# Delta-rule attention: the merge's first and second products in steps of their own, and stage_d by kind of product

## The chip, the cores and the metric

The kernel runs on one core of one Trainium2 chip. The metric is the device time in microseconds of one execution; before the change the median of three runs is 844.51 us (843.97 to 844.6). Engines are named as in the profile: PE multiplies matrices, PEld loads its weights, DVE and ACT do elementwise work, POOL fills memory, SP issues most transfers.

## The reference

Three parts follow one another: a delta-rule attention over 4 batches, 8 heads, 768 positions and head size 48; a block with Fourier transforms and a two-layer network; and a gated block. Only the first is touched:

```python
k_n = k / (np.linalg.norm(k, axis=-1, keepdims=True) + 1e-06)
state = np.zeros((B, H, D, D), dtype=np.float32)
for t in range(S):
    kt, vt, bt = (k_n[:, :, t], v[:, :, t], beta[:, :, t, None])
    y[:, :, t] = np.einsum('bhd,bhde->bhe', q[:, :, t], state)
    v_old = np.einsum('bhde,bhd->bhe', state, kt)
    state = state + bt[:, :, :, None] * np.einsum('bhd,bhe->bhde', kt, vt - v_old)
```

## The kernel before, in words

Attention is done in chunks of 64 positions. There are 12 chunks for each of 4 batches, 48 pairs of batch and chunk, called bc, in an order in which batches overlap. A loop over steps t = -3 to 47 runs several stages for different bc in one step:

- `stage_a(t + 20)` (L220, while there are chunks left) multiplies keys with keys and queries into the buffer `gak` of that chunk; ACT (L199, L200) and DVE (L702) copy it there.
- The solver (generator `solve`, on DVE) inverts the triangular matrices of a block of 8 chunks. `part(f)` lets it go on until a share of its work is done, so a block's work is spread over 8 steps. Its last instructions are two transposes (L346) into `Tc`, which holds the inverses of the two 32 x 32 diagonal quarters of each 64 x 64 matrix.
- `merge` builds the remaining quarter for two chunks, number g (chunks 2g and 2g + 1). Its 16 first products (L467) multiply the keys' products in `gak` with `Tc` into PSUM; ACT copies the result, negated, to `ZS` (L471). Its 16 second products (L469) multiply `Tc` with `ZS`, and ACT copies them to `TT` (L474 twice). In an odd step t, with g = (t + 3) / 2, the call `merge(g + 1, ...)` issues the second products of g interleaved with the first products of g + 1. The first products of a block's first merge (g a multiple of 4) stand alone, at t = 5, 13, 21, ..., after stage_d; there the second products of t = 3, 11, 19, ... stand alone too.
- After the first products of a merge have read `gak`, `load_kv` overwrites that part with the chunk's keys and values. `values(bc)` then scales the values, on DVE (L488) for even bc and on ACT (L491) for odd bc.
- `stage_b(t + 2)` (L498) multiplies `TT` with keys and values; ACT copies the result to `WU` (L500).
- `stage_c(t + 1)` (L513) corrects the queries, and DVE subtracts them into `cw` (L515).
- `stage_d(t)` (L533 and L534) adds products with the solved values `WU` and, unless the chunk is a batch's first, products with the corrected queries `cw` and the state `Sb` into two PSUM banks, for each of 4 pairs of heads in turn; ACT copies the state (L542) and the output (L551 twice).

`chain()` at the end of a step fixes the order of instructions on each engine as written. So every engine works through its own list in order, and a wait of one instruction holds back all behind it on that engine. Every fp32 product is two PE instructions in the trace (an x32 there is 16 products). "Light" steps are those from t = 37 on: the solver is done, and transforms of finished batches (`dft`) and conversions of weights fill in. In these, SP also brings in the transforms' tables (`in_sc`, `in_dc`) and, one a step from t = 24, weights of 384 KB.

The lines that the change touches are L523 to L534 (stage_d), L642 and L646 (the start of a step) and L674 to L679 (the odd step's merge and its loads).

Of the kernel before, what the change touches and what calls it, by code (L numbers as in the profile page):

```python
# [20 lines left out]
C = 64  # L21
NC = S // C
HP = H // 2
NBC = B * NC
# [42 lines left out]
class Kernel:  # L67
# [51 lines left out]
    def attention(self, cp, pg, pe, p, x, filler, after_solves):  # L119
        nc, a, load = self.nc, self.a, self.load  # L120
# [12 lines left out]
        hs, ds = (slice(0, C), slice(C, 2 * C)), (slice(0, D), slice(C, C + D))  # L133
# [313 lines left out]
        light = lambda t: t >= 8 * NB - 11  # L447
# [9 lines left out]
        def merge(g8, first, second):  # L457

            z0, z1 = zz[:, g8 % 2 * 256 : g8 % 2 * 256 + 256].rearrange("p (g n) -> p g n", g=8), zz.rearrange("p (g n) -> p g n", g=8)
            T0, o0 = (Tts[g8 // 4] if first else None), (g8 % 4) * 8  # L460
            T1, o1 = (Tts[(g8 - 1) // 4] if second else None), ((g8 - 1) % 4) * 8
            tt = TT[(g8 - 1) % NTT]
            for g in range(8):
                for h in range(2):
                    if first:
                        ga = gas[g8 * 2 + g // 4][:, g % 4]
                        nc.tensor.matmul(z0[lo[h], g], lhsT=ga[up[h], C : C + 32], rhs=T0[up[h], o0 + g], start=True, stop=True)  # L467
                    if second:
                        nc.tensor.matmul(z1[up[h], g], lhsT=T1[lo[h], o1 + g], rhs=ZS[(g8 - 1) % 2][lo[h], g], start=True, stop=True)  # L469
            if first:  # L470
                nc.scalar.mul(ZS[g8 % 2][:96, :, 32:], z0[:96], -1.0)  # L471
            if second:
                for h in range(2):
                    nc.scalar.copy(out=tt[lo[h], :, C * h : C * h + C], in_=z1[up[h]])  # L474


        def load_kv(bc):
            load(out=gas[bc][:, :, C:], in_=a["kv"][bc])
# [5 lines left out]
        def values(bc):  # L484
            kv = gas[bc][:, :, C:]
            if light(bc - 2) or bc >= 8 and bc % 2 == 0:
                n = n_all[:, bc * 4 : bc * 4 + 4].unsqueeze(2).to_broadcast([128, HP, D])
                nc.vector.tensor_tensor(out=kv[:, :, D:], in0=kv[:, :, D:], in1=n, op=MUL)  # L488
                return
            for hp in range(HP):  # L490
                nc.scalar.activation(kv[:, hp, D:], kv[:, hp, D:], AF.Copy, scale=n_all[:, bc * 4 + hp : bc * 4 + hp + 1])  # L491

        def stage_b(bc):
            kv = gas[bc][:, :, C:]
            tt, o = TT[(bc // 2) % NTT], (bc % 2) * 4
            pb = self.bank("pb", [128, HP, 2, D])
            for hp in range(HP):
                nc.tensor.matmul(pb[:, hp].rearrange("p t d -> p (t d)"), lhsT=tt[:, o + hp], rhs=kv[:, hp], start=True, stop=True)  # L498
            wu = WU[bc % NWU]
            nc.scalar.copy(out=wu, in_=pb.rearrange("p h t d -> p h (t d)"))  # L500
            st[bc] = [wu, None]
# [16 lines left out]
        def stage_d(bc):  # L518

            b, c = SEQ[bc]  # L520
            wu, cw = st.pop(bc)
            sb = Sb[b]
            po, ps = self.bank("pd", [128, HP, D]), None  # L523
            if c < NC - 1:
                ps = self.bank("pd", [128, HP, D])
            for hp in range(HP):
                for last in (False, True)[: 1 + (c > 0)]:
                    end = last == (c > 0)
                    for i, h in enumerate(hs):

                        k, u, n = (cw[ds[i], hp], sb[ds[i], hp], C + D) if last else (gas[bc][h, hp], wu[h, hp, D:], 2 * C)
                        if ps is not None:
                            nc.tensor.matmul(ps[C * i : C * i + n - C, hp], lhsT=k[:, C:n], rhs=u, start=not last, stop=end)  # L533
                        nc.tensor.matmul(po[hs[1 - i], hp], lhsT=k[:, :C], rhs=u, start=not last, stop=end)  # L534
            if c == HALF:
                px = self.bank("pb", [128, HP, 2, D])
                xr = p.tile([1, DM], F32, name="xr", bufs=2)
                for i in range(2):
                    for hp in range(HP):
                        nc.tensor.matmul(px[C * i : C * i + 1, hp, i], lhsT=qx[ds[i], b, hp : hp + 1], rhs=sb[ds[i], hp], start=True, stop=True)  # L540
            if c < NC - 1:
                nc.scalar.copy(out=sb, in_=ps)  # L542
            if c == HALF:
                for i in range(2):
                    nc.scalar.copy(out=xr.rearrange("p (h t d) -> p h t d", h=HP, t=2)[:, :, i], in_=px[C * i : C * i + 1, :, i])
                st["x", b] = xr
            cc = c if c < HALF else NC - 1 - c
            js = slice(64 * (cc % 2), 64 * (cc % 2) + 64)
            tl = cc // 2 + (0 if c < HALF else 3)
            for i in range(2):  # L550
                nc.scalar.copy(out=x[b][js, tl].rearrange("p (h t d) -> p h t d", h=HP, t=2)[:, :, i], in_=po[hs[1 - i]])  # L551
            if c == NC - 1:
                nc.scalar.copy(out=x[b][0:1, 3], in_=st.pop(("x", b)))
# [77 lines left out]
        for t in range(T0, NBC):  # L631
            if t in STARTS:
                if solver:
                    solver.finish()
                j, span, total = STARTS[t]
                solver, since = Spread(solve(j), total), t
            part = (lambda f: solver.upto(SECOND(t + f) if j == 1 else (t - since + f) / span)) if solver and not light(t) else (lambda f: None)
            if light(t) and solver:
                solver.finish()
                solver = None  # L640

            if 0 <= t + 2 < NBC and (not light(t) or (t + 2) % 8 == 0):  # L642
                values(t + 2)
            for bc in ahead.get(t, ()):
                mask_q(bc)
            part(c1)  # L646
            if t >= 0:
                stage_d(t)
                if SEQ[t][1] == NC - 1:
                    fill.extend(filler(SEQ[t][0]))  # L650
            new = t % 8 == 5 and t + 3 < NBC
            if new:

                merge((t + 3) // 2, True, False)
                load_kv(t + 3)
                load_kv(t + 4)
                diag((t + 3) // 2)
            corrected = stage_c(t + 1) if 0 <= t + 1 < NBC else iter(())
            if t + R + 2 < HEAD or HEAD <= t + R < NBC:
                stage_a(t + R + 2 * (t < 4), corrected)  # L660
            for _ in corrected:
                pass
            if light(t + 1) and t + 3 < NBC and (t + 3) % 8:
                values(t + 3)
            part(c2)
            odd = t % 2 and (t + 3) // 2 < NBC // 2
            if t == NBC - 12:
                solver.finish()
                loads, tail = after_solves()
            if t % 2 == 0 and t % 8 != 4 and t + 4 < NBC:  # L670
                diag((t + 4) // 2)
            if (odd or light(t + 1)) and 0 <= t + 2 < NBC:
                stage_b(t + 2)
            if odd:  # L674
                g = (t + 3) // 2
                merge(g + 1, (g + 1) % 4 > 0, True)
                if (t + 5) % 8 and t + 5 < NBC:
                    load_kv(t + 5)
                    load_kv(t + 6)  # L679
            if light(t + 1):  # L680

                for _ in range(CF["dfs"][t - (NBC - 12)]):
                    while fill and next(fill[0], 1) == 1:
                        fill.pop(0)
                for _ in range(CF["cvt"][t - (NBC - 12)]):
                    next(tail, None)
            elif not odd and 0 <= t + 2 < NBC:
                stage_b(t + 2)
            if 2 <= t + 4 < NBC:
                load_qt(t + 4)  # L690
            if t == -2:
                right(2)
                left(2)
            if t == -1:
                right(3)
            if t == 0:
                left(3)
            part(1)

            while late:  # L700
                out, m0, m1 = late.pop()
                nc.vector.tensor_tensor(out=out, in0=m0, in1=m1, op=MUL)  # L702
            self.chain()
            next(loads, None)
            if t >= NBC // 2:
                next(self.words, None)
            self.chain()
# [753 lines left out]
```

## Time and profile before

| what | value |
|---|---|
| median of 3 runs | 844.51 us |
| the profiled execution's own time | 842.8 us |
| its span, first to last instruction | 841.0 us |
| PE busy | 807.8 us (96%) |
| DVE busy | 599.6 us (71%) |
| ACT busy | 408.9 us (49%) |
| mean granted clock | 0.974 |

Attention takes about the first 265 us. A busy PE in this table is one that has some instruction in flight; matmuls are pipelined, so how long a stage takes is read from its start to the start of the next one. In timeline rows the first number is the start and the second how long a run of like instructions lasted; what stands in brackets is how long the engine was idle before it and who ended that.

### The profile page before, as it was taken

What the parts mean: (1) busy time and instruction counts of PE and PEld (TensorE: products, weight loads), DVE (VectorE), ACT (ScalarE), POOL (GpSimd) and SP (SyncE); (2) the same over time, 40 slices, a digit from 0 to 9 for tenths busy, and PEclk for the clock granted to TensorE, in tenths of its full rate; (3) what the DMA queues carried; (4) which work ended last, traced back from release to release, by engine and by line L of the source; (5) the groups of instructions that cost most, each with busy time, mean ns of one, the idle gap of its engine ahead of it and who ended that gap; (6) DMA issues with size and microseconds to landing.
All of it is one profiled execution on the core that took longest, in us unless ns stands there. A gap on an engine that the chain in (4) does not pass through costs nothing.

```text
span 841.0 us, 24593 instructions
## 1 busy us (share of the span) xinstructions
PE 807.8 (96%) x10291; PEld 770.3 (92%) x10291; DVE 599.6 (71%) x1715; ACT 408.9 (49%) x1026; POOL 7.6 (1%) x60
## 2 busy tenths in 40 slices
PE   7898898889999999999999999999999999999998
PEld 7788787878988999899999999999899899899998
DVE  6988779999978995682935983345678477586663
ACT  3668868878665543232232551233452553543632
POOL 1000000000000000000000000000000000000000
PEclk9769979999999999999999999999999999999999
DMA  9634444456624200000114310112001101102001
GB/s 232 175 92 125 139 122 133 110 171 175 180 80 147 103 0 2 0 13 18 42 32 124 98 34 15 48 55 66 20 9 45 62 15 43 57 25 70 21 1 57
DMA packets 56417, 62.10 MB, mean 74 GB/s; under 512 B 31665, under 2 KB 48786, under 8 KB 56306
## 3 DMA queue, kind: packets, MB, share of 16 engines
q1 hardware_dynamic: 56162, 60.38, 24.6%
q8 instruction: 81, 1.33, 0.7%
q14 instruction: 30, 0.25, 0.1%
q10 hardware_dynamic: 144, 0.15, 0.1%
HBM read 48.12 MB, written 4.72 MB: 63 GB/s over the span
## 4 chain that ended last, share of the span: by engine, by line
PE 83%; DVE 11%; issue 2%; DMA 2%; ACT 1%; SPq 0%; ACTq 0%; DVEq 0%
PE bankX L946 17%; PE bankY L959 15%; PE bankX L1144 10%; PE bankX L1124 6%; PE bankX L1092 6%; PE bankY L1172 5%; PE bankY L498 4%; PE bankX L220 3%; PE bankY L533 2%; PE bankY L513 2%; PE bankV L959 2%; PE bankX L759 2%; PE bankY L534 2%; DVE cw L515 1%; PE bankZ L469 1%
## 5 line engine op out<-in xcount | busy, mean ns | idle before, releaser
L959 PE MATMUL bankY<-w,hx 128*128 128x384 f32 x756 | 147.2, 337 | 0.0
L946 PE MATMUL bankX<-uh,w 128*128 128x384 f32 x504 | 137.8, 340 | 0.7 <-DVE ul L868 0.7
L959 PEld LDWEIGHTS bankY<-w,hx 128*128 128x128 f32 x756 | 132.4, 188 | 0.5 <-issue 0.3
L951 DVE SCALAR_TENSOR_TENSOR hx<-bankX,hx 128x384 fp32r<-128x384 f32 x84 | 46.3, 552 | 74.4 <-ACT hx L950 71.9
L950 ACT ACTIVATE hx<-bankX 128x384 fp32r<-128x384 f32 x84 | 41.2, 490 | 109.6 <-PE bankX L946 105.2
L946 PEld LDWEIGHTS bankX<-uh,w 128*128 128x128 f32 x504 | 92.2, 188 | 1.2 <-DVE ul L868 0.9
L1144 PE MATMUL bankX<-w,A 128*128 128x384 f32 x504 | 88.8, 335 | 0.0
L1144 PEld LDWEIGHTS bankX<-w,A 128*128 128x128 f32 x504 | 87.6, 188 | 0.0
L946 PE MATMUL bankX<-ul,w 128*128 128x384 f32 x252 | 85.1, 338 | 0.0
L498 PE MATMUL bankY<-gak,TT 128*128 128x96 f32 x384 | 58.7, 299 | 5.3 <-DVE gak L488 1.9
L498 PEld LDWEIGHTS bankY<-gak,TT 128*128 128x128 f32 x384 | 50.5, 204 | 14.2 <-issue 2.8
L534 PE MATMUL bankY<-WU,gak 64*64 64x48 f32 x768 | 52.1, 231 | 0.0
L1124 PE MATMUL bankX<-xh,s 128*128 128x384 f32 x192 | 50.0, 338 | 0.0
L534 PE MATMUL bankY<-Sb,cw 48*64 48x48 f32 x704 | 47.5, 226 | 2.0 <-issue 2.0
L1133 ACT CAST u<-hx 128x384 fp32r<-128x384 f32 x32 | 15.8, 513 | 67.6 <-DVE hx L1131 67.6
L220 PE MATMUL bankX<-kq 48*64 48x128 f32 x640 | 48.0, 298 | 0.5 <-issue 0.5
L946 PEld LDWEIGHTS bankX<-ul,w 128*128 128x128 f32 x252 | 47.4, 188 | 0.0
L533 PE MATMUL bankY<-Sb,cw 48*48 48x48 f32 x640 | 38.8, 211 | 8.8 <-DVE cw L515 6.4
L513 PE MATMUL bankY<-gak,WU 64*64 64x112 f32 x704 | 46.0, 270 | 1.3 <-issue 1.3
L1092 PE MATMUL bankX<-s,xh 128*128 128x512 f32 x144 | 45.9, 395 | 0.0
L533 PE MATMUL bankY<-WU,gak 64*64 64x48 f32 x704 | 44.9, 232 | 0.6 <-ACT gak L200 0.6
L533 PEld LDWEIGHTS bankY<-WU,gak 64*64 64x64 f32 x704 | 37.5, 141 | 4.9 <-issue 1.0
(240 smaller groups left out, 1846.9 us busy)
## 6 DMA issues: line engine op xcount, KB each, us to landing
qt<-in_qt_dram SPq DMA_DIRECT2D x48, 196.0 KB, 3.4
gak<-in_kv_dram SPq DMA_DIRECT2D x48, 192.0 KB, 3.8
w<-in_w_dram SPq DMA_DIRECT2D x24, 384.0 KB, 5.6
kq<-in_kc_dram SPq DMA_DIRECT2D x20, 448.0 KB, 4.1
out_dram<-x SPq DMA_DIRECT2D x24, 192.0 KB, 1.9
x<-x SPq DMA_DIRECT2D x96, 36.0 KB, 1.9
s<-in_wi_dram SPq DMA_DIRECT2D x6, 512.0 KB, 4.3
un<-xh SPq DMA_DIRECT2D x80, 36.0 KB, 1.9
```

The costliest lines, as they stand in the source:

```text
L220: nc.tensor.matmul(pa[q, hp], lhsT=kq[r, hp, C:], rhs=kq[r, hp], start=True, stop=True)
L498: nc.tensor.matmul(pb[:, hp].rearrange("p t d -> p (t d)"), lhsT=tt[:, o + hp], rhs=kv[:, hp], start=True, stop=True)
L513: nc.tensor.matmul(pc[h, hp], lhsT=w[h, hp, :C], rhs=gas[bc][h, hp, : C + D], start=True, stop=True)
L533: nc.tensor.matmul(ps[C * i : C * i + n - C, hp], lhsT=k[:, C:n], rhs=u, start=not last, stop=end)
L534: nc.tensor.matmul(po[hs[1 - i], hp], lhsT=k[:, :C], rhs=u, start=not last, stop=end)
L946: nc.tensor.matmul(ph, lhsT=w1[f][i][:, c * 128 : c * 128 + 128], rhs=cur[k][:, c], start=(c + j == 0), stop=(c == 2 and j == 2))
L951: nc.vector.scalar_tensor_tensor(out=hl, in0=ph, scalar=0.0, in1=hh.bitcast(F32), op0=MAX, op1=SUB)
L959: nc.tensor.matmul(acc[t], lhsT=hx[i][:, t * 128 : t * 128 + 128], rhs=w2[e][k], start=(e == 0 and j == 0), stop=(e == 11 and j == 2),)
L1092: nc.tensor.matmul(pv, lhsT=xT[t][i][:, c, kk * 128 : kk * 128 + 128], rhs=wi[2 * c + 1][k], start=(c + j == 0), stop=(c == 2 and j == 2))
L1124: nc.tensor.matmul(pu, lhsT=wi[2 * c][i][:, f * 128 : f * 128 + 128], rhs=xT[hf][k][:, c], start=(c + j == 0), stop=(c == 2 and j == 2))
L1144: nc.tensor.matmul(acc, lhsT=A[:, m, o, i, kk], rhs=Bo[name, kk][:, k], start=(kk + j == 0), stop=(kk == 2 and j == 2))
L1172: nc.tensor.matmul(po, lhsT=a[:, :128], rhs=wo[f][k], start=(f + j == 0), stop=(f == last and j == 2))
```

## The change

In odd steps `merge` is now called for its second products alone. The first products of the merges that don't begin a block move to the end of the even step before, behind stage_b, and the two loads of keys and values behind them with them. stage_d issues all heads' products with the solved values, then all heads' products with the corrected queries, as one accumulation group of a bank. The solver's part at the start of a block's last step is left out, so that it is done in the same step's later parts. For even chunks that don't begin a block, `values` is written at the end of a step instead of the start of the next.

```diff
+        def sooner(bc):
+            return 8 <= bc < NBC and bc % 8 in (2, 4, 6) and not light(bc - 2)
...
-            for hp in range(HP):
-                for last in (False, True)[: 1 + (c > 0)]:
-                    end = last == (c > 0)
+            for last in (False, True)[: 1 + (c > 0)]:
+                for hp in range(HP):
+                    begin, end = (not last and hp == 0, last and hp == HP - 1) if c else (True, True)
                     for i, h in enumerate(hs):
...
-                            nc.tensor.matmul(ps[C * i : C * i + n - C, hp], lhsT=k[:, C:n], rhs=u, start=not last, stop=end)
-                        nc.tensor.matmul(po[hs[1 - i], hp], lhsT=k[:, :C], rhs=u, start=not last, stop=end)
+                            nc.tensor.matmul(ps[C * i : C * i + n - C, hp], lhsT=k[:, C:n], rhs=u, start=begin, stop=end)
+                        nc.tensor.matmul(po[hs[1 - i], hp], lhsT=k[:, :C], rhs=u, start=begin, stop=end)
...
-            if 0 <= t + 2 < NBC and (not light(t) or (t + 2) % 8 == 0):
+            if 0 <= t + 2 < NBC and (not light(t) or (t + 2) % 8 == 0) and not sooner(t + 2):
                 values(t + 2)
...
-            part(c1)
+            if t - since < span - 1:
+                part(c1)
...
             if odd:
                 g = (t + 3) // 2
-                merge(g + 1, (g + 1) % 4 > 0, True)
-                if (t + 5) % 8 and t + 5 < NBC:
-                    load_kv(t + 5)
-                    load_kv(t + 6)
+                merge(g + 1, False, True)
...
             elif not odd and 0 <= t + 2 < NBC:
                 stage_b(t + 2)
+            if t % 2 == 0 and t % 8 != 4 and t + 4 < NBC:
+                merge((t + 4) // 2, True, False)
+                load_kv(t + 4)
+                load_kv(t + 5)
             if 2 <= t + 4 < NBC:
                 load_qt(t + 4)
...
+            if sooner(t + 3):
+                values(t + 3)
             self.chain()
```

On PE, from the end of step t = 13 into t = 14, before: stage_b, the interleaved merge, then stage_d of a batch's first chunk.

```order
L498 MATMUL bankY<-gak,TT_90 128x96 x4
L467 MATMUL bankZ<-Tc,gak 32x32
L469 MATMUL bankZ<-ZS_84,Tc 32x64
L467 MATMUL bankZ<-Tc,gak 32x32
L469 MATMUL bankZ<-ZS_84,Tc 32x64
...
L533 MATMUL bankY<-WU_91,gak 64x48
```

And now, from the end of step t = 14 to the end of t = 15 (lines are those of the changed file, where stage_d is L537 and L538, stage_c L516 and stage_b L501):

```order
L501 MATMUL bankY<-gak,TT_89 128x96 x4
L467 MATMUL bankZ<-Tc,gak 32x32 x16
L537 MATMUL bankY<-WU_92,gak 64x48
L538 MATMUL bankY<-WU_92,gak 64x48
...
L537 MATMUL bankY<-Sb_93,cw 48x48
L538 MATMUL bankY<-Sb_93,cw 64x48
...
L501 MATMUL bankY<-gak,TT_89 128x96 x4
L469 MATMUL bankZ<-ZS_85,Tc 32x64 x16
```

First products now have a run of their own behind stage_b in even steps, second products in odd steps, and in stage_d all 16 products on `WU` precede the first on `Sb`.

On DVE, at a block's turn (end of the solver's block at t = 12), before and then now:

```order
L702 TENSOR_TENSOR gak<-bankX,mk 128x4x64
L488 TENSOR_TENSOR gak<-gak,n_all 128x4x48
L346 STREAM_TRANSPOSE Tc<-Ts 128x16x32 x2
L515 TENSOR_TENSOR cw<-qt,bankY 112x448
L702 TENSOR_TENSOR gak<-bankX,mk 128x4x64
```

```order
L708 TENSOR_TENSOR gak<-bankX,mk 128x4x64
L488 TENSOR_TENSOR gak<-gak,n_all 128x4x48
L518 TENSOR_TENSOR cw<-qt,bankY 112x448
L346 STREAM_TRANSPOSE Tc<-Ts 128x16x32 x2
L708 TENSOR_TENSOR gak<-bankX,mk 128x4x64
```

cw has moved ahead of the two transposes; at two later turns (t = 20 and 28) it moves ahead of the first of them alone. Elsewhere DVE's order is what it was.

On SP, around t = 37 and 38, before and then now (gak: keys and values, qt: queries, s: the transforms' tables, w: weights of the second part):

```order
L105 DMA s_4902<-in_sc_dram 128x1281
L105 DMA gak<-in_kv_dram 128x4x96 x4
L105 DMA qt<-in_qt_dram 112x448
L105 DMA s_4903<-in_dc_dram 97x386
L105 DMA w_3_5056<-in_w_dram 128x768
L105 DMA qt<-in_qt_dram 112x448
```

```order
L105 DMA s_4902<-in_sc_dram 128x1281
L105 DMA gak<-in_kv_dram 128x4x96 x2
L105 DMA qt<-in_qt_dram 112x448
L105 DMA s_4903<-in_dc_dram 97x386
L105 DMA w_3_5037<-in_w_dram 128x768
L105 DMA gak<-in_kv_dram 128x4x96 x2
L105 DMA qt<-in_qt_dram 112x448
```

The loads of chunks 42 and 43 now stand behind the table of 97 rows and a weight.

## Rows read from the trace of the kernel before

**Rows 1.** The page: PE's busy tenths and granted clock in 40 slices.
```profile
PE   7898898889999999999999999999999999999998
...
PEclk9769979999999999999999999999999999999999
```

**Rows 2.** Windows: length, busy us of PE, PEld, DVE, ACT, POOL; clock; DMA.
```profile
31.00:54.90 23.90, 23.09 (x589) 20.57 (x589) 23.27 (x101) 13.69 (x43) 0.15 (x1) 0.54 0.39 108
...
80.00:100.00 20.00, 18.05 (x688) 16.10 (x681) 17.18 (x64) 17.10 (x51) 0.00 (x0) 1.00 0.57 164
...
150.00:190.00 40.00, 35.86 (x1256) 32.19 (x1252) 38.71 (x146) 32.98 (x98) 1.08 (x11) 1.00 0.54 150
...
212.00:240.00 28.00, 27.94 (x848) 25.52 (x843) 22.09 (x64) 18.80 (x47) 0.00 (x0) 1.00 0.61 176
```

**Rows 3.** The chain of waits by line, from 85, 150 and 212 us.
```profile
by line: PE bankY L498 18.5%; PE bankX L220 14.5%; PE bankY L533 12.2%; PE bankY L534 10.7%; PE bankY L513 9.2%; DVE Cc L253 8.5%; issue 8.3%; PE bankZ L469 7.4%; DVE Ts L260 5.5%; DVE cw L515 2.7%; PE bankY L540 2.6%; PE bankZ L467 2.4%
...
by line: DVE cw L515 11.0%; DVE tm L300 10.4%; issue 8.8%; DVE Ts L297 8.7%; DVE gak L702 7.4%; DVE tm L314 7.4%; DVE tm L290 7.2%; DVE Ts L295 6.9%; DVE Cc L253 6.6%; DVE Ts L329 6.3%; DVE tm L325 4.9%; DVE Tc L346 3.3%; DVE gak L488 2.7%;
...
by line: PE bankY L498 23.4%; PE bankY L513 17.0%; PE bankX L759 13.1%; PE bankY L533 12.9%; PE bankZ L469 9.8%; PE bankY L534 9.4%; PE bankZ L467 5.1%; PE bankX L753 2.6%; PE bankX L755 2.4%; PE bankY L540 2.1%; ACT w L841 1.9%; issue 1.4%
```

**Rows 4.** Windows of whole merges, L469 alone: length, PE, PEld; clock; DMA.
```profile
153.66:154.69 1.03, 1.02 (x32) 0.93 (x32) 1.00 0.17 37
144.69:145.70 1.01, 1.01 (x32) 0.92 (x32) 1.00 0.26 30
...
118.26:120.12 1.86, 1.85 (x32) 1.69 (x32) 0.50 0.43 159
```

**Rows 5.** The same view of L467 alone, where first products stand alone.
```profile
184.81:185.43 0.62, 0.62 (x32) 0.58 (x32) 1.00 0.75 202
...
113.42:114.41 0.99, 0.99 (x32) 0.92 (x32) 0.50 0.00 0
```

**Rows 6.** Timeline of PE: two waits before 108 us.
```profile
84.42 0.26 PE L533 MATMUL bankY<-WU,gak 64*64 64x48 f32 x2 [0.58 <-ACT gak L200]
...
92.24 0.31 PE L513 MATMUL bankY<-gak,WU 64*64 64x112 f32 x1 [1.29 <-issue]
```

**Rows 7.** Timeline of DVE at the turn after t = 12.
```profile
109.29 1.95 DVE L346 STREAM_TRANSPOSE Tc<-Ts 128x512 f32<-128x512 f32 x2
111.10 0.59 DVE L515 TENSOR_TENSOR cw<-qt,bankY 112x448 f32<-112x448 f32 x1
```

**Rows 8.** Timeline of PE there: stage_d(13) and the first products behind it.
```profile
111.74 0.31 PE L533 MATMUL bankY<-Sb,cw 48*48 48x48 f32 x1 [0.75 <-DVE cw L515]
...
113.42 1.06 PE L467 MATMUL bankZ<-Tc,gak 32*32 32x32 f32 x32
```

**Rows 9.** Timeline of PE: waits in steps 32 and 43.
```profile
202.68 0.80 PE L498 MATMUL bankY<-gak,TT 128*128 128x96 f32 x6 [0.62 <-ACT x L551]
...
245.63 0.24 PE L533 MATMUL bankY<-Sb,cw 48*48 48x48 f32 x1 [0.54 <-DVE cw L515]
```

**Rows 10.** Timeline of ACT in the odd step t = 5.
```profile
81.09 0.39 ACT L471 ACTIVATE ZS<-bankZ 96x256 f32<-96x256 f32 x1
```

**Rows 11.** The page, costliest groups: L533's two kinds (busy, mean ns, idle before).
```profile
L533 PE MATMUL bankY<-Sb,cw 48*48 48x48 f32 x640 | 38.8, 211 | 8.8 <-DVE cw L515 6.4 <-issue 2.3
...
L533 PE MATMUL bankY<-WU,gak 64*64 64x48 f32 x704 | 44.9, 232 | 0.6 <-ACT gak L200 0.6
```

**Rows 12.** Transfers issued from 160 to 200, then 221.5 to 227.4 us.
```profile
gak<-in_kv_dram SPq DMA_DIRECT2D x10, 192.0 KB, 4.1
...
gak<-in_kv_dram SPq DMA_DIRECT2D x2, 192.0 KB, 8.1
```

**Rows 13.** Timelines of DVE and PE: chunk 42 in steps 39 and 40.
```profile
226.06 0.35 DVE L488 TENSOR_TENSOR gak<-gak,n_all 128x192 f32<-128x192 f32 x1
...
228.56 1.13 PE L498 MATMUL bankY<-gak,TT 128*128 128x96 f32 x8
```

**Rows 14.** A window ahead of the clock's fall, as in rows 2.
```profile
102.00:109.50 7.50, 6.18 (x228) 5.34 (x219) 4.73 (x8) 5.44 (x17) 0.67 (x8) 1.00 0.48 146
```

## The prediction

> **What bounds the kernel now.** I read the page first, for the granted clock over the span: it is at full speed but for a few slices in the first third of the span, the attention stage, which is all that the change touches [rows 1]. Then the busy time of each engine in stretches of that stage [rows 2]. Two regimes show. From 31 to 108 us and again from 212 to 240 us PE is the fullest engine (23.09 of 23.90, 18.05 of 20, 27.94 of 28); from 150 to 190 us DVE is, with 38.71 of 40, and PE has 4 us to spare there. The chain of waits says the same by what it runs through [rows 3]: PE's stage lines between 85 and 108 and between 212 and 240 us, the solver's DVE lines between 150 and 180 us. So time added on PE counts in the first and the last of these stretches, and hardly in the middle; and nothing after attention is changed, where the page's row of PE is all but full [rows 1], so a delay at the end of attention stays.
>
> **The two kinds of merge products.** A merge has 16 first and 16 second products, two PE instructions each. Where both kinds are interleaved the pair takes 1.03 us from its start to the next stage; where second products stand alone (steps t = 3, 11, ...) they take 1.01 us [rows 4], and first products alone (t = 5, 13, ...) 0.62 us [rows 5]. The first products, in other quarters of the array, ride along for 0.02 us. Split, the two cost 1.01 + 0.62 = 1.63 us: +0.60 us of PE for each pair at full clock. At half clock the interleaved pair takes 1.86 us [rows 4] and first products alone 0.99 us [rows 5]; second products alone are not shown at that clock. If they take the pair's time, as they do at full clock, the split costs +0.99 there; if they take less, not under the 0.60. I take 1.0. By the code there are 18 such pairs (g = 1 to 23 without the multiples of 4). In the order of the program:
>
> - Before 108 us: g = 1, 2, 3, 5, 6, 7. The first two fall into the stretch with clock 0.54 [rows 2]: 1.0 + 0.8 (g = 2 has other small products beside it). g = 3, 6, 7: 0.6 each. g = 5: its first products come to stand at the end of t = 6, ahead of stage_d(7), where PE waits 0.58 us for ACT anyway [rows 6]: 0. Sum 3.6. PE also stands still there with nothing the profile names, 1.29 us at 92 us the longest I show [rows 6]. If its instructions simply come too slowly, a longer merge with the same instructions soaks into that: I take off 1.0, between 0 and 1.3. Left: +2.6.
> - The block's turn, 108 to 122 us: g = 9 at half clock, +1.0. Against it stands the skipped solver part at t = 12: cw of step 13 now goes ahead of the two Tc transposes instead of behind them [rows 7]. PE's wait of 0.75 us for that cw [rows 8] goes. Next late is Tc for the first products at 113.42: cw first, the pair of transposes ends at 109.29 + 0.59 + 1.95 = 111.8, still ahead of stage_d's end at 113.42 - 0.75 = 112.7. So -0.75. Net +0.2.
> - 122 to 190 us: g = 10, 11, 13, 14, 15, together 3.0 us of PE in a stretch where PE has 4 us left in 40 and DVE 1.3 [rows 2]. DVE's order is the same there apart from one transpose that changes places with cw at two turns. 0; if PE's slack lies in the wrong steps, up to +2.
> - 190 to 246 us: g = 17, 19, 21, 22 at 0.6 each. g = 18: at the end of t = 32, where stage_b has just waited 0.62 us for ACT's copies [rows 9]; ACT's queue is shorter by the ZS product in odd steps (below), so 0.6 - 0.4 = 0.2. g = 23: at the end of t = 42, before stage_d(43), which waits 0.54 us for cw anyway [rows 9]: 0.1. Sum +2.7.
>
> **ACT.** The ZS product (0.39 us) leaves its place ahead of the two TT copies in odd steps [rows 10] and goes behind stage_b's copy in even ones. It is the same work; where the chain runs through ACT, before the 0.58 us wait of stage_d(7), it is -0.4.
>
> **stage_d.** Each of the 44 steps with corrected queries now issues all 32 instructions on WU and then all 32 on Sb. The mean durations differ little (232 and 211 ns on L533 [rows 11]) and the tiles are the same, so I count the stage's own length as unchanged; no row shows the Sb kind alone, and 0.03 us either way in the 25 or so steps on PE's path would be 0.8. What it saves is the wait for cw: more products now stand ahead of the first that needs it. Those waits are in DVE's stretch, where DVE sets the end, or already spent on first products above: 0.
>
> **The loads of kv.** The load of bc and bc + 1 moves from the end of step bc - 5 to that of bc - 4, because the first products of g = bc / 2 must read the old contents. The first reader is DVE's multiplication L488 one step later, and in DVE's order that has not moved. A kv load takes 4.1 us in the busy middle [rows 12], and a step there about 4.5 (the starts 144.69 and 153.66 in rows 4 are two steps apart): DVE still reaches L488 after the landing. The place to watch is bc = 42. On SP its load used to go out ahead of the odd transfer of 97 rows (s from in_dc) and of a 384 KB weight; now it stands behind both. What stands behind that transfer lands late: the kv loads issued between 221.5 and 227.4 us take 8.1 us [rows 12]. On the other hand the 97 rows themselves no longer queue behind that kv load and start sooner, by my estimate the better part of a step, 3 us, so I take 8.1 - 3 = 5.1 us. L488 wants the data at 226.06 [rows 13], a stage_d and the products of stage_c after the end of t = 38; so the load goes out at 223.4 by my estimate and lands at 228.5. L488 is then at 226.06 plus the 1.0 that PE is later there. DVE waits 1.4 us, and the products of the transforms and stage_b(42) at 228.56 [rows 13] come behind it: +1.4. Ends: 0 (it takes 4.1 us) and 4.4 (8.1 us). In a sentence by itself: the Trainium skill (DMA: Bandwidth & Descriptors, "Why a DMA increments its semaphore by 16 and not by 1") says that a transfer is split over the largest number up to 16 that divides its slowest dimension, so 97 rows go through one engine; the trace agrees in that the transfers around it take twice as long, and by the rule alone the wait would be towards the upper end.
>
> **Sum.** 2.6 + 0.2 + 0 + 2.7 - 0.4 + 0 + 1.4 = +6.5 us on the profiled execution, 842.8 us (span 841.0): 849.3. The median of the runs shown is 1.7 above that execution, so 851.0.
>
> **Rivals.** *Even steps have room* (not slower). PE's waits before 108 us lie in even steps behind ACT, whose odd steps are the heavier; with ZS moved, both get even, and the first products vanish into waits everywhere, not at two places only. Then what remains is -0.75, -0.4 and the second of those waits, -0.6, with no split cost and no late load: -1.8, 842.7. For it: the 0.58 and 0.62 us waits [rows 6, 9]. Against it: PE's 27.94 of 28 [rows 2], where there is no wait to vanish into. It decides if fewer than a third of the pairs cost their 0.6.
>
> *The clock stays up at the turn* (about no change). The granted clock was full up to 109.5 us, in a stretch in which PE was busy for 6.18 of 7.5 us [rows 14], and at 113 and 118 us it is 0.50 [rows 4, 5]. PE works some 9 us there that would take 5 by the pair's 1.86 and 1.03 us. With cw earlier and more PE work in even steps the lull is shorter; if the clock doesn't fall, -4 and g = 9 costs 0.6 instead of 1.0: 846.6. Against it: most of the lull is PE waiting for ACT and DVE's block work, which stays. By the Trainium skill (TensorE: Matmul & The Clock Gate, Part 1) the gate follows how busy PE has been of late; the trace agrees, with the fall behind the emptiest stretch in that region.
>
> *The kv load is the bound* (slower yet). Landing after 8.1 us, and waits of under 1 us in other even steps as the weights share the queue: +3 more, 854.0.
>
> *The split does nothing else than it says, but costs in DVE's stretch too*: +2, 853.0.
>
> **How the numbers follow.** The forecast, 848 to 853 by its own bounds, has 0.50; even steps with room 0.15; the clock 0.12; kv 0.13; DVE's stretch 0.10. For 8 in 10 the range goes from the first rival to past the third: 843 to 856. Runs of this kernel tell a change of 0.2%, 1.7 us, from none. Faster takes most of the first rival, a part of the clock's and a little of the forecast: 0.20; same 0.14; slower 0.66.
>
> **What would show it.** In the profile after: every merge on its own, 1.01 and 0.62 us; PE busier by some 0.6 us a pair between 60 and 108 and between 212 and 240 us, with no new idle time; the wait of stage_d(13) for cw gone; DVE idle before L488 near 227 us with the kv load named. I am wrong if first products turn out to stand where PE waited before, if stage_d in its new order is shorter than 64 interleaved instructions, or if the half clock at 109 us is gone or another one has come.

## The result, and the profile after

The changed kernel takes 858.35 us, the median of 17 runs (848.41 to 864.93), the kernel before on the same chip 844.86. The ratio of the two is 1.0116, with a 95% interval of 1.0087 to 1.0145; such a ratio leaves out disturbed runs (here two of the 17, in E6 below one of 1969.83 us among others), so it is less than the quotient of the medians, 1.016. On the 844.51 us shown ahead of the prediction it makes 854.3 us (851.9 to 856.8). The profiled execution took 860.47 us, its span is 858.7 us, at the upper end of the runs. All ratios below are to the kernel before on the same chip, with such an interval.

The page of the changed kernel, in the slices of [rows 1]:

```profile
PE   7899899999898999999999999999999999999998
...
PEclk9769889999959999999999999999999999999999
```

The granted clock has a new hole in the 12th slice, 236 to 258 us. Just ahead of it, near 233 us, is the wait that the prediction named. Timelines of DVE, then of PE:

```profile
227.82 0.61 DVE L518 TENSOR_TENSOR cw<-qt,bankY 112x448 f32<-112x448 f32 x1
233.12 0.36 DVE L488 TENSOR_TENSOR gak<-gak,n_all 128x192 f32<-128x192 f32 x1 [4.69 <-DMA gak<-in_kv_dram]
233.40 0.55 DVE L747 TENSOR_TENSOR s<-s 128x384 f32<-128x384 f32 x1
```

```profile
230.95 0.46 PE L516 MATMUL bankY<-gak,WU 64*64 64x112 f32 x6
233.74 1.10 PE L501 MATMUL bankY<-gak,TT 128*128 128x96 f32 x8 [2.33 <-DVE gak L488]
235.19 0.51 PE L761 MATMUL bankX<-s,s 128*97 128x65 f32 x2 [0.35 <-DVE s L749]
```

DVE reaches the scaling of chunk 42's values (L488) and stands 4.69 us for its load; behind it wait the additions of the transforms (L747 to L749) and, on PE, stage_b (L501) and the transforms' products (L761). PE stops for 2.33 us. In [rows 13] the same L488 has no wait at all. Then windows of the changed kernel, with the columns of [rows 2]:

```profile
225.00:231.40 6.40, 6.40 (x234) 5.73 (x233) 3.37 (x13) 3.94 (x9) 0.00 (x0) 1.00 0.69 194
231.40:233.70 2.30, 0.01 (x1) 0.00 (x0) 0.58 (x2) 1.00 (x4) 0.00 (x0) 1.00 0.66 209
233.70:235.00 1.30, 1.10 (x8) 0.97 (x8) 1.23 (x3) 0.07 (x1) 0.00 (x0) 1.00 0.10 36
235.00:255.00 20.00, 19.79 (x218) 17.98 (x220) 7.43 (x17) 6.55 (x17) 0.00 (x0) 0.51 0.15 43
```

PE is full up to 231.4, empty for 2.3 us, and from 235 us on the clock is at its half level for 20 us, although PE is full again. What this costs is read from ACT's output copies of steps 40 and 41, before (L551) and after (L555):

```profile
229.43 0.64 ACT L551 COPY x<-bankY 64x192 f32<-64x192 f32 x2
234.73 0.31 ACT L551 COPY x<-bankY 64x192 f32<-64x192 f32 x1
```

```profile
231.82 0.64 ACT L555 COPY x<-bankY 64x192 f32<-64x192 f32 x2
245.41 0.64 ACT L555 COPY x<-bankY 64x192 f32<-64x192 f32 x2
```

Up to step 40, behind 16 split merges, this execution is 2.4 us late in all; one step later it is 10.7 us, and at step 42, by the same copies, 15.5. About 1 us of these 13.1 also comes in E6 below, where PE does not stop (its step 41 takes 6.29 us, before 5.30). So in this execution the place of chunk 42 costs some 12 us.

The merges themselves are as forecast: windows of L467 alone, then of L469 alone, at full and at half clock (beside [rows 4, 5]):

```profile
210.08:210.70 0.62, 0.62 (x32) 0.58 (x32) 1.00 0.11 26
...
240.55:241.54 0.99, 0.99 (x32) 0.93 (x32) 0.50 0.00 0
```

```profile
213.51:214.53 1.02, 1.02 (x32) 0.92 (x32) 1.00 0.85 272
248.08:249.93 1.85, 1.85 (x32) 1.67 (x32) 0.50 0.27 92
```

### The profile page after: what moved, and what is told of

It reads as the page before. It is cut to its first block, busy times and chain, and to the rows that moved or that the text cites. A ratio compares the mean times of both kernels' runs of the same rounds, so it can differ in the third digit from the quotient of the medians.

```text
span 858.7 us, 24588 instructions
## 1 busy us (share of the span) xinstructions
PE 828.8 (97%) x10291; PEld 789.6 (92%) x10291; DVE 599.4 (70%) x1715; ACT 409.2 (48%) x1026; POOL 7.6 (1%) x60
## 4 chain that ended last, share of the span: by engine, by line
PE 82%; DVE 11%; ACT 3%; issue 2%; DMA 1%; POOL 0%; ACTq 0%; DVEq 0%; POOLq 0%
PE bankX L954 17%; PE bankY L967 15%; PE bankX L1152 10%; PE bankX L1132 6%; PE bankX L1100 6%; PE bankY L1180 5%; PE bankX L220 3%; PE bankY L501 3%; PE bankX L767 2%; PE bankV L967 2%; PE bankZ L469 2%; PE bankY L537 2%; PE bankY L516 2%; DMA gak<-in_kv_dram 1%; PE bankY L538 1%
## 5 line engine op out<-in xcount | busy, mean ns | idle before, releaser
L501 PE MATMUL bankY<-gak,TT 128*128 128x96 f32 x384 | 58.5, 298 | 6.3 <-DVE gak L488 3.5
L501 PEld LDWEIGHTS bankY<-gak,TT 128*128 128x128 f32 x384 | 50.3, 204 | 15.2 <-issue 5.6
L516 PE MATMUL bankY<-gak,WU 64*64 64x112 f32 x704 | 47.5, 273 | 3.3 <-issue 3.0
L220 PE MATMUL bankX<-kq 48*64 48x128 f32 x640 | 50.0, 305 | 0.0
L518 DVE TENSOR_TENSOR cw<-qt,bankY 112x448 f32<-112x448 f32 x44 | 27.0, 613 | 22.1 <-PE bankX L220 14.4
L220 PEld LDWEIGHTS bankX<-kq 48*64 48x64 f32 x640 | 41.5, 153 | 0.6 <-issue 0.2
L516 PEld LDWEIGHTS bankY<-gak,WU 64*64 64x64 f32 x704 | 37.4, 140 | 4.9 <-issue 4.5
L1180 PE MATMUL bankY<-s,u 128*128 128x384 f32 x160 | 39.8, 337 | 0.0
L538 PE MATMUL bankY<-WU,gak 64*64 64x48 f32 x768 | 35.6, 233 | 0.2 <-issue 0.2
```

Of the source, the lines that this page charges most:

```text
L220: nc.tensor.matmul(pa[q, hp], lhsT=kq[r, hp, C:], rhs=kq[r, hp], start=True, stop=True)
L516: nc.tensor.matmul(pc[h, hp], lhsT=w[h, hp, :C], rhs=gas[bc][h, hp, : C + D], start=True, stop=True)
L1180: nc.tensor.matmul(po, lhsT=a[:, :128], rhs=wo[f][k], start=(f + j == 0), stop=(f == last and j == 2))
```

## The experiments

Theory A: the late load of chunk 42, and the half clock behind PE's stop, are most of the loss. Theory B: the split merges are. Theory C: transfers there are slow in general. The clock falls at other places too, and not at the same ones in each execution of one kernel, so single executions differ by some us; verdicts rest on ratios, and profiles only on what stands at chunk 42.

**E1 and E10: the changed kernel, the table in two transfers.**

```diff
-                self.load(out=self.dc, in_=a["dc"])
+                self.load(out=self.dc[:96], in_=a["dc"][:96])
+                self.load(out=self.dc[96:], in_=a["dc"][96:])
```

> The changed kernel with the table of 97 rows loaded in two transfers, of 96 rows and of 1 row; nothing else differs. Theory A (the late load): the load of chunk 42 is late because the 97 rows go as a chain of small packets ahead of it, and PE's wait there is what the half clock of 235 to 256 us follows. Then the load's time falls from 7.5 to 4 to 5 us, DVE's wait of 4.69 us before L488 shrinks to under 1.5, the half clock there goes, and the kernel comes to 846 to 849 us, 2 to 4 over the kernel before. Theory B (the split merges are the price, and the wait and the half clock cost nothing of their own): it stays at 855 to 860. Theory C (all transfers there are slow because of the weights): the load still takes over 6 us and DVE still waits over 3 us.

> E1's kernel once more (the table in two transfers), since its six runs came to +1.0% although its profile has no wait for chunk 42, and E6, which takes the same wait away in another way, came to +0.2%. Theory A: chance of the granted clock in few runs; now 849 to 853, a ratio of 1.001 to 1.006. Theory B (something else in that order of transfers costs time outside the profiled execution): 1.008 or more again.

Measured: 855.89 us, ratio 1.0101 (1.0063 to 1.014), from 6 runs; again, from 12 runs, 853.42 us, 1.005 (1.0014 to 1.0085). In the first profile DVE does not wait at chunk 42's L488, in the second it waits 2.03 us, as its timeline has it:

```profile
235.90 0.36 DVE L488 TENSOR_TENSOR gak<-gak,n_all 128x192 f32<-128x192 f32 x1 [2.03 <-DMA gak<-in_kv_dram]
```

PE stops for it in neither, and in neither does the clock fall between 232 and 258 us. What was expected at the place came; the first ratio did not, and it spoke for theory B until E6. What the first profile lost, it lost earlier: by the output copies its step 36, ahead of the table's rows, is already 9.4 us later than in the profile of the changed kernel, and two windows of it are partly at half clock where the changed kernel has 1.00:

```profile
60.00:80.00 20.00, 20.00 (x463) 18.10 (x463) 10.11 (x18) 12.02 (x38) 0.92 (x10) 0.60 0.35 90
...
125.00:150.00 25.00, 23.81 (x616) 21.79 (x614) 19.14 (x90) 16.31 (x47) 0.00 (x0) 0.75 0.52 136
```

The second ratio is half the first. The load, behind the table and the weight, takes 3.5 us in the one and 5.2 in the other, so this mend is not a sure one.

**E2: the kernel before with the same two transfers**, as a control.

> The kernel before with the same table in two transfers. Theory A: its load of chunk 42 stands ahead of the table, so nothing waits for it: within 1 us of the kernel before (844 to 845), and what E1 gains is not a gain that any kernel would get. Theory B gives the same. If it becomes faster by 2 us or more, the table costs the kernel before something too, and E1 has to be read against this run.

Measured: 848.61 us, ratio 1.0025 (0.9998 to 1.0051). It brings no gain of its own.

**E3: the kernel before with chunk 42 late, and nothing else.**

```diff
-                if (t + 5) % 8 and t + 5 < NBC:
+                if (t + 5) % 8 and t + 5 < NBC and t != 37:
...
+            if t == 38:
+                load_kv(42)
+                load_kv(43)
```

> The kernel before with one edit: the loads of chunks 42 and 43 are issued a step later, at the end of t = 38, behind the table of 97 rows and a weight, as in the changed kernel. No merge is split. Theory A: DVE waits 3 to 5 us before L488 near 227 us with the load named, PE waits 2 us or more, and the clock falls to half for 10 to 20 us: 852 to 858 us. Theory B: under 1 us more than before. If the wait comes but the clock stays up: 846 to 848.

Measured: 854.13 us, ratio 1.0095 (1.0066 to 1.0124). No merge is split, and nearly the whole loss is there. Its transfers, its DVE, its PE and its windows show the same chain:

```profile
gak<-in_kv_dram SPq DMA_DIRECT2D x2, 192.0 KB, 10.0
```

```profile
237.60 0.36 DVE L488 TENSOR_TENSOR gak<-gak,n_all 128x192 f32<-128x192 f32 x1 [4.72 <-DMA gak<-in_kv_dram]
```

```profile
238.22 1.15 PE L498 MATMUL bankY<-gak,TT 128*128 128x96 f32 x6 [2.29 <-DVE gak L488]
```

```profile
235.90:238.20 2.30, 0.03 (x2) 0.01 (x1) 0.60 (x2) 1.38 (x4) 0.00 (x0) 1.00 0.46 112
238.20:245.00 6.80, 6.78 (x32) 6.17 (x32) 5.81 (x13) 0.96 (x2) 0.00 (x0) 0.54 0.43 128
```

The load takes 10.0 us, PE stops 2.29 us, and the clock is at half for the next 6.8. From the output copies of step 40 to those of step 41 it is 11.16 us, before 5.30; the step after is as long as before (8.75):

```profile
236.71 0.64 ACT L551 COPY x<-bankY 64x192 f32<-64x192 f32 x2
247.87 0.31 ACT L551 COPY x<-bankY 64x192 f32<-64x192 f32 x1
```

So the trace puts the stop and the half clock behind it at 5.9 us: 2.29, and half of some 7. By the ratio the loss is 8 us, between 5.6 and 10.5.

**E7: E3 with the table in two transfers.**

> E3 again (the kernel before with the loads of chunks 42 and 43 a step later, behind the table and a weight), but with the table in two transfers, of 96 rows and of 1 row. If the chain of 97 rows is what makes the load late: no wait before L488 and within 2 us of the kernel before, where E3 was 8 over it. If the place behind the weight is enough: a wait of 2 us or more and 850 or more.

Measured: 849.09 us, ratio 1.0001 (0.9976 to 1.0025). The load of chunk 42, still behind the table and the weight, now takes 4.9 us:

```profile
gak<-in_kv_dram SPq DMA_DIRECT2D x2, 192.0 KB, 4.9
```

E3's loss is gone. So it was the 97 rows in one transfer, not the place behind a weight: theory C falls.

**E4: the split alone, in place.** The kernel before, where a merge issues its first products and then its second products.

```diff
-            for g in range(8):
-                for h in range(2):
-                    if first:
...
-                    if second:
+            for kind in range(2):
+                for g in range(8):
+                    for h in range(2):
+                        if first and kind == 0:
...
+                        if second and kind == 1:
```

> The kernel before with one edit: where a merge issues both kinds of products interleaved, it issues all 16 first products and then all 16 second products, in the same place. This is the price on PE of 18 pairs no longer interleaved, with no load moved. The prediction's terms (0.6 us a pair in PE's stretches, nothing between 122 and 190 us) give about +6 us, 851. Theory A, which gives most of the loss to the load, leaves +2 to +3: 847 to 848. If a pair in two runs still takes 1.03 us, 844.5.

Measured: 851.54 us, ratio 1.0045 (1.0018 to 1.0073), some +3.8 us. A pair in two runs takes 1.43 us, as a window of the merge at 221.87 us has it:

```profile
221.87:223.30 1.43, 1.43 (x64) 1.00 0.86 225
```

That is 0.40 over the interleaved 1.03 [rows 4], not 0.60: 18 times 0.40 is 7.2 us, of which about half shows. It lies between the 2 to 3 us of theory A and the 6 of the prediction.

**E5: the changed kernel again**, beside E6 to E8.

> The changed kernel as it is, on the same chip and beside the same runs of before as the two below, so that each of its parts has a measure of the whole. Ratio 1.008 to 1.015 expected by every theory, since nothing is changed.

Measured: 858.57 us, ratio 1.011 (1.0064 to 1.0155). The profiled execution, 852.45 us, is the shortest of the six. In it PE stops 2.24 us at the same L501, and the clock is at half for 7 us behind it, where it was 20 in the first profile:

```profile
232.50:239.50 7.00, 6.96 (x39) 6.19 (x41) 5.80 (x13) 1.04 (x3) 0.00 (x0) 0.54 0.04 14
```

**E6 and E11: the changed kernel, the table and the weights a step later**, behind chunk 42.

```diff
+                yield
                 self.load(out=self.dc, in_=a["dc"])
```

> The changed kernel with the table of 97 rows (in one transfer, as it is) and the weights behind it issued one step later, behind the loads of chunks 42 and 43 instead of ahead of them. Theory A (the late load and the fall of the clock behind it are most of the loss): the load takes about 4 us, no wait of DVE before L488 near 227 us, no half clock at 235 to 256 us, and 3 us or more faster than E5. Theory B (the split merges are most of the loss, and E1 stayed at +1.0% for that reason): within 2 us of E5, though the wait is gone.

> E6's kernel once more, beside its control E12. E6's interval (0.999 to 1.0056) leaves open whether the split merges cost anything once chunk 42 is in time. If the products in even steps take only time in which PE stood still: 0.999 to 1.003. If they cost the prediction's 5 us: 1.005 or more.

Measured: 850.78 us, ratio 1.0023 (0.999 to 1.0056); again 851.44 us, 1.0035 (0.9998 to 1.0071). The load of E6, its L488, and a window of E6 over the stretch that was at half clock:

```profile
gak<-in_kv_dram SPq DMA_DIRECT2D x2, 192.0 KB, 3.5
```

```profile
229.10 0.36 DVE L488 TENSOR_TENSOR gak<-gak,n_all 128x192 f32<-128x192 f32 x1 [0.44 <-DMA gak<-in_kv_dram]
```

```profile
239.00:258.00 19.00, 18.59 (x454) 16.92 (x455) 13.67 (x33) 11.75 (x29) 0.00 (x0) 1.00 0.29 87
```

With every merge split and the table whole, but chunk 42 in time, 1.1% has become 0.2 to 0.4%. Theory A holds: by the ratios some 6 to 8 of the 9 to 10 us are the load. DVE's wait alone is not the price: at 241.88 us of the same profile it waits 2.88 us for chunk 44's load, and PE does not stop. Whether the split merges cost anything then is not decided: E11's 1.0035 lies between the two values expected, 1.003 and 1.005, and its interval holds both.

**E12: the kernel before with that edit**, as a control.

> The kernel before with E6's edit alone: the table of 97 rows and the weights behind it one step later. Nothing waits for them there in either trace, so 0.998 to 1.002. If it is faster by 2 us or more, E6 and E11 have to be read against it, and the edit is a gain for both kernels.

Measured: 849.56 us, ratio 0.9992 (0.9958 to 1.0026). It brings no gain of its own.

**E8: stage_d by kinds and the skipped solver part, alone, on the kernel before**; the two edits are those of the change's diff.

> The kernel before with two parts of the change alone: stage_d by kinds of products, and the solver's part at the start of a block's last step left out. No merge is split and no load moved. By the prediction the wait of stage_d(13) for cw goes (-0.75) and stage_d costs nothing: 0 to -1 us, not to be told from the kernel before by its time. If stage_d by kinds is slower or faster by 0.03 us a step: 0.8 us either way. If these two parts are the loss: +3 or more.

Measured: 846.99 us, ratio 0.9996 (0.9963 to 1.003). These two parts cost nothing that these runs can tell, at most some 2.5 us.

**E9: the changed kernel with chunk 42's scaling a step later on DVE.**

```diff
-            if light(t + 1) and t + 3 < NBC and (t + 3) % 8:
+            if light(t + 1) and t + 3 < NBC and (t + 3) % 8 and t != 39:
                 values(t + 3)
...
+            if t == 40:
+                values(42)
             if (odd or light(t + 1)) and 0 <= t + 2 < NBC:
```

> The changed kernel with the scaling of chunk 42's values (L488) written a step later on DVE, just ahead of the stage_b that reads them. No load is moved, so the load is as late as in the changed kernel (about 7.5 us). Theory A (what hurts is not the slow load but that DVE, in order, stands before L488 and holds the products of the transforms and stage_b on PE): the transforms' additions and cw go ahead, the wait at L488 shrinks to under 1.5 us, PE does not stop for 2.3 us, no half clock follows, 848 to 852 us as E6. If the chain of 97 rows slows everything around it by its own: 856 to 860 as E5.

Measured: 853.33 us, ratio 1.0066 (1.0034 to 1.0097), between E5 and E6, and not for the reason expected. The profiled execution, 862.03 us, is one of the longest of the twelve, and in it the load of chunk 42 takes 3.7 us, not 7.5, so it does not test the edit against a late load. No wait stands at L488, but PE stops all the same. DVE, PE and the windows of E9:

```profile
240.83 0.56 DVE L756 SCALAR_TENSOR_TENSOR s<-s,s 128x384 f32<-128x384 f32 x1
241.31 0.61 DVE L518 TENSOR_TENSOR cw<-qt,bankY 112x448 f32<-112x448 f32 x1
241.84 0.35 DVE L488 TENSOR_TENSOR gak<-gak,n_all 128x192 f32<-128x192 f32 x1
242.20 0.59 DVE L453 COPY TT<-Tc 32x256 f32<-32x256 f32 x2
242.82 0.36 DVE L488 TENSOR_TENSOR gak<-gak,n_all 128x192 f32<-128x192 f32 x1
```

```profile
243.44 0.83 PE L501 MATMUL bankY<-gak,TT 128*128 128x96 f32 x3 [2.69 <-DVE gak L488]
```

```profile
240.70:243.40 2.70, 0.04 (x2) 0.00 (x0) 2.61 (x8) 1.04 (x4) 0.00 (x0) 1.00 0.66 186
243.40:247.00 3.60, 3.56 (x18) 3.59 (x19) 1.17 (x3) 0.48 (x1) 0.00 (x0) 0.53 0.00 0
```

The first L488 is chunk 43's (from chunk 39 on DVE scales every chunk, the odd ones too), the second chunk 42's. DVE is busy for all of PE's stop (2.61 of 2.70 us): chunk 42's L488 now stands behind the transforms' additions, cw, chunk 43's L488 and a copy, so stage_b waits for work in DVE's queue. No transfer is named there, and the clock falls to half all the same. My expectation that L488 could be put off for nothing was wrong.

No kernel here beats the kernel before: E12 and E8 are nearest, and the intervals of both hold no change. Not tested alone are the other loads of keys and values, a step later in the change, and the values written earlier for some even chunks.

## The prediction, step by step

The sign and the reason for it in general (PE is the bound, a delay at the end of attention stays) held, and the range too by the ratio (854.3 us), though the median of those runs lies above it. The sum did not come about as it was added up: two steps erred in opposite directions. The split, with the block's turn and ACT, was put at 5.1 us, and E6 and E11 leave 2 to 3 by their middle values; the load was put at 1.4, and the ratios give 6 to 8.

- **What bounds the kernel**: right. 2.33 us of PE standing still at 231 us were never won back; step 47 is 16.3 us late, the span 17.7 us longer. One reading was wrong: in the row for 31 to 54.9 us [rows 2] DVE is fuller than PE, 23.27 against 23.09.
- **The price of a merge**: right to 0.01 us, 0.62 and 1.02 at full clock; the open one, second products alone at half clock, is the pair's time, 1.85 against 1.86 [rows 4].
- **What the split costs on PE's path**: this step failed. +2.6, +2.7 and the -0.4 of ACT were forecast. Between the output copies of steps 29 and 40, a stretch without half clock in any of the three, the windows are, of the kernel before, of the changed one and of E6:

```profile
185.38:229.43 44.05, 42.07 (x1368) 37.84 (x1362) 41.48 (x155) 32.53 (x87) 0.15 (x1) 1.00 0.64 183
```

```profile
187.81:231.82 44.01, 42.64 (x1329) 38.59 (x1322) 38.25 (x148) 32.10 (x85) 0.16 (x1) 1.00 0.61 175
```

```profile
188.03:231.85 43.82, 42.93 (x1332) 38.96 (x1326) 40.76 (x154) 32.03 (x86) 0.15 (x1) 1.00 0.58 163
```

The stretch is as long as before: 44.05, 44.01 and 43.82. The same windows of the merges' tile alone, before and in E6:

```profile
185.38:229.43 44.05, 7.58 (x392) 1.00 0.64 183
```

```profile
188.03:231.85 43.82, 10.08 (x360) 1.00 0.58 163
```

The merges do take 2.5 us more, four times 0.6 as forecast. But PE's idle time falls from 1.98 to 0.89 us: the wait for ACT (0.62 us [rows 9]) and 0.85 us of "issue" (nothing named) in a stage_d at 206 us are gone. So 1.1 of it is covered. The rest is not explained: from start to start the instructions of stage_b and stage_d take about 1.3 us less in this stretch of E6, in E8 they don't, and no run separates that. It is not one execution's luck: in E1, E5, E10 and E11, without half clock too, the stretch takes 43.9 to 44.7 us. In E4, where the two runs stand in one place, it takes 46.56: there five pairs at 0.40 are paid. Between steps 1 and 10 it is 40.78 us before and 40.69 after, again nothing, where the terms for g = 3, 5, 6 and 7 less the soak make 0.8. The terms for g = 1 and 2 can't be read: the changed kernel is 2.2 us late at step 1, but so is E8, by 2.7, without a split merge. I had read the window with 27.94 of 28 us as if the whole of 190 to 246 were so, and had set only 0.6 for waits; steps 29 to 36 had almost 2 us of them.
- **stage_d(7) waits for nothing new** (g = 5 at no cost): wrong, and the 0.4 us taken off for ACT at this place did not come either. Its wait grew from 0.58 us [rows 6] to 1.38, and the profile names the ZS copy, which now stands in ACT's queue in the even step:

```profile
85.26 0.34 PE L537 MATMUL bankY<-WU,gak 64*64 64x48 f32 x2 [1.38 <-ACT ZS L471]
```

- **The block's turn**: +0.2 forecast; from step 10 to step 14 it is 21.76 us before and 21.79 after. The 0.75 us wait for cw is gone as said. The half clock has moved ahead and is shorter, 6.6 us at clock 0.50 from 105.8 us, but PE stood still for 2.06 us ahead of it; so what the skipped solver part brings there can't be read from these two executions. E8 says that it is little. The half clock did not go away, as the rival on the clock had it.
- **122 to 190 us**: 0, with up to +2; steps 14 to 28 took 58.99 us before and 59.97 after. **stage_d**: 0, and E8 has 0.
- **The load of chunk 42**: the place, the instruction and the mechanism were right, the size was not. Forecast were a load issued at 223.4 that takes 5.1 us and a wait of 1.4. It was issued at 225.63, took 7.5, and DVE waited 4.69:

```profile
gak<-in_kv_dram SPq DMA_DIRECT2D x2, 192.0 KB, 7.5
```

I had taken off 3 us because the table would start sooner. It was issued at 221.37 but its rows went from 224.3 to 230.4 us, behind the transfers of the step before (in the kernel before from 223.6 to 230.4); the 8.1 us of [rows 12], the upper end, was the better value. The rule that I had set aside for the sum, of the Trainium skill (DMA: Bandwidth & Descriptors, "Why a DMA increments its semaphore by 16 and not by 1"), by which 97 rows go through one engine, pointed to the upper end; E3 and E7, 10.0 against 4.9 us with 97 against 96 and 1 rows, agree with it.
- **What had no term at all**: the clock behind the wait. That "another half clock has come" stood in the prediction as something that would make it wrong, without a price. The step that failed is the price of a wait: I counted PE's stop as the time it stands still. In E3, where nothing else is changed, the stop is 2.29 us, the step with it 5.9 us longer, and the loss by the ratio 8 us (0.66 to 1.24%).

Of the rivals, "the kv load is the bound" was the nearest in what happened and in the time, 854.0 us, at a chance of 0.13; its +3, on top of the forecast's 1.4, should have been some +5 to +7. "Even steps have room" was nearer on the merges than the forecast was, but not right (2 to 3 us by the middle values of E6 and E11, where it had a gain), and wrong as a whole, because the late load came with it. That the total fell into the range, and on the rival's 854.0, is luck: the sum of the two errors. What stays open is why E1 and E10, without the stop on PE, were still 0.5 to 1.0% slower, more than E6 and E11: their lowest clocks lie at other places in the profiles, and no experiment ties these to the edit. The mean granted clock of their runs was lower (0.965 and 0.968, with 0.974 and 0.973 for the kernel before beside them), that of E6 and E11 was not (0.971 and 0.972, beside 0.972).

## What to carry to other kernels

When a change moves a load in a queue, look at what it now stands behind: one transfer of an odd shape can hold up all that follow, and an engine that works in order passes the wait on to whatever is queued behind. Price a stop of a full TensorE not at its length but with what the clock may do afterwards: in E3's profile two and a half times as much. And before counting added PE work at its full price, add up PE's idle time over just those steps, not over a neighbouring window; here that accounts for 1.1 of 2.5 us.

## What the runs showed of the hardware

- **The half clock after a stop.** In four profiles PE, full until then, stood still for 2.2 to 2.7 us near step 41 (the changed kernel, E3, E5, E9), and in each the granted clock went to half (0.51 to 0.54 over the windows shown) within 2 us of PE's return, for 20, 7, 7 and 3.5 us. In the profiles of the other kernels, before among them, it was at full speed from step 39 to step 43. Shorter stops went both ways: behind 1.62 us in E7, at 231 us, the clock stayed up; behind 1.37 us in E9, at 229.7 us, it was at half for 3.4 us. How long it stays down was not to be foreseen: the same kernel had 20 us once and 7 us once. What PE waited for was not the same in all four: a transfer behind DVE in three, DVE's own queue in E9.
- **A transfer of 97 rows.** Its rows took 6.1 us, at some 26 GB/s. The changed kernel's page of 224 to 231 us, in 40 slices, shows that rate alone for a while:

```profile
GB/s 294 318 272 272 149 167 105 44 26 26 26 18 26 26 120 26 18 152 202 202 288 242 255 213 294 272 146 96 126 246 302 303 385 256 259 360 307 284 342 331
```

The weight issued right behind it took 10.7 us, in E7 4.5.
- **Interleaving on PE.** 16 small first products took 0.62 us alone; a run of them with the second products right behind cost 0.40 more than the two interleaved (E4's 1.43 less 1.03), and interleaved the two took 0.02 more than second products alone.
